# Block 0's second product by seven half products, and a new written order of all work

## The chip, the cores and the metric

The kernel runs on one core of one Trainium2 chip. The metric is the device time of one execution in microseconds; lower is better. The engines are named as in the profile: PE (TensorE matmul; PEld is its weight load), DVE (VectorE), ACT (ScalarE), POOL (GpSimd) and SP (SyncE). Each runs its own instructions in the order in which they are written.

## What is computed

An attention with a window, followed by a two-layer network with a squared ReLU:

```
scores = q @ k.T / sqrt(64) - slope[h] * dist        # 4 batches, 8 heads, 768 positions
keep   = (pos_k < 8) | (0 <= pos_q - pos_k < 96)     # global keys, and a local window
a      = softmax(where(keep, scores, -1e9))
x      = (a @ v), heads side by side                 # 3072 tokens x 512
out    = relu(x @ w_in) ** 2 @ w_out                 # w_in 512 x 2048, w_out 2048 x 512
```

## The kernel before

The 3072 tokens are 24 tiles of 128 (index j), six to a batch. Two tiles make a block (`blk`, 0 to 11). Matmuls run in bf16 and accumulate in eight PSUM banks.

For each tile: loads of q, k and v (q and k of tile 0 come by SP); transposes `tr.n.j` on PE with copies `T.n.j` for tiles 0 to 7, and transposing DMAs for later ones; scores `sc.j` (with a bias matmul `bias.j` for tiles 0 to 2); `exp.j` on ACT; the mask's product `mul.j` on DVE; `pv.j.0` and `pv.j.1`, which multiply by v; `norm.j.0` and `norm.j.1` on DVE, which divide by the row sums; and the transpose of the result, `trx.j` on PE with the copy `xT.j`. `gk`, `gv` and `kl` are small copies of the eight global keys and values.

The first product, x by w_in, has 8 steps of 256 hidden columns. Blocks 0 and 1 do it directly (`s1.blk.s`, L1061; then `relu` and `sq`). For block 0 the steps 0 to 3 are cut by token tile, and steps 0 and 2 also by column half, whose weights are loaded in two pieces, so that `s1.0.0` has four quarters. Blocks 2 to 11 do it by a Strassen-like scheme of seven half products p1 to p7 for each of two groups of steps (`h.blk.g.pN`, L950), with sums of weights `isum` (L888), sums of tokens `xs`, copies `u`, output additions `c` (L995) and squares `q`.

The second product, the squared hidden values by w_out, is direct for block 0 (`s2.0.s.sub`, L1339: 32 matmuls of 512 columns into two banks) and by seven half products for blocks 1 to 11 (`s2.blk.pN.g`, L1212: 8 matmuls of 256 columns for each). The seven-product form needs differences of w_out (`wsum.i.g`, L1132, where g is the half of w_out's steps), sums of the squared hidden values (`sum.blk.i`, L1167), copies of partial results (`part`) and output additions (`o.blk.pN`, L1287). Its banks are two: x takes p1, p6, p7 and p4, and y takes p2, p5 and p3.

Two sets name the blocks that take the seven-product forms:

```
SEVEN = set(range(1, NBLK))      # second product
SEVEN1 = set(range(2, NBLK))     # first product
```

The whole program is laid down in the order of a long string, `ORDER`. Each word is one piece of work; `@A`, `@V` or `@P` picks ACT, DVE or POOL, and `:` gives the PSUM banks. Since every engine works through its own instructions in order, the string sets each engine's queue. On POOL's queue stand the loads (`ld.win.s.c` and `ld.wout.s` for pieces of the weights, `ld.q.j`, `ld.k.j`, `ld.v.j` for tiles 1 to 5, and `load.j` for all three parts of a later tile). SP's queue has the stores and the transposing DMAs.

Of the kernel before, what the change touches and what calls it, by code (L numbers as in the profile page):

```python
# [58 lines left out]
tr.0.1:1 ld.v.0 exp.0.1.0 T.0.1@V sc.1.0 exp.1.0.1 pv.0.0:2 ld.q.2 tr.0.2:3 norm.0.0 ld.k.2 T.0.2@V ld.k.3 exp.1.1.1
pv.0.1:4 tr.1.2:1 bias.2.0:7203 ld.v.1 norm.0.1 exp.1.1.0 ld.q.3 tr.1.3:6 gk.1@A T.1.2@A sc.2.0 exp.1.0.0 T.1.3@V  # L60
ld.k.4 pv.1.0:4 ld.v.2 gk.2@V exp.2.1.0 exp.2.1.1 norm.1.0 trx.0:1 xT.0@A ones.6 pv.1.1:5 tr.0.3:6 T.0.3@V exp.2.0.0
tr.1.4:2 ld.win.6.0 sc.3.0:4361 ld.q.4 norm.1.1 ld.v.3 trx.1:7 gv.1@V exp.2.0.1 exp.3.0.0 pv.2.0:5 exp.3.1.0 exp.3.0.1
T.1.4@V xT.1@V pv.2.1:0 ld.k.5 ld.win.2.0 exp.3.1.1 gk.3@A ld.win.2.1 norm.2.0 s1.0.3:2 mul.3.0 s1.0.6:4 ld.win.4.0
tr.0.4:7 ld.q.5 ld.v.4 norm.2.1 mul.3.1 relu.0.6@A s1.0.3#2 gv.2@P pv.3.0:3 norm.3.0 trx.2:5 T.0.4@A pv.3.1:6
ld.win.1.0 norm.3.1 ld.win.0.1 xT.2@A sc.4.0:1047 exp.4.1.1 exp.4.1.0 tr.1.5:3 T.1.5@A s1.0.2:5 trx.3:6 xT.3@V
ld.win.0.0 ld.win.5.0 s1.0.2#2 s1.0.2#3 s1.0.2#4 relu.0.3@V exp.4.0.1 ld.v.5 gv.3@P exp.4.0.0 gk.4@V sq.0.6@V
relu.0.2@A s1.1.3:7 ld.win.7.0 relu.1.3@A load.6 s1.1.6:0 mul.4.1 tr.0.5:6 mul.4.0 sq.0.3@V s1.1.2:3 T.0.5@A ld.wout.3
pv.4.0:2 ld.wout.1 sq.0.2@V sc.5.0:4157 ld.wout.0 s1.0.4:6 relu.1.2@A exp.5.1.1 s1.0.1:3 sq.1.3@A exp.5.0.0 relu.0.4@V
s1.1.4:7 ld.wout.2 norm.4.0 pv.4.1:4 gv.4@P norm.4.1 sq.0.4@A load.7 exp.5.1.0 sq.1.2@A relu.1.4@A s1.0.0:6 gate.9
ld.wout.4 mul.5.0 s1.0.0#2 sq.1.4@A s1.0.0#3 s1.1.5:2 trx.4:1 exp.5.0.1 relu.1.6@V s1.1.1:4 ld.wout.5 s1.0.1#2  # L70
relu.1.1@A E0.1 mul.5.1 relu.1.5@A pv.5.0:7 s1.1.7:0 s1.1.0:5 sq.1.1@V norm.5.0 ld.wout.6 E0.0 sq.1.5@V tr.1.6:4
sq.1.6@A pv.5.1:2 relu.1.7@A tr.0.6:7 s1.0.0#4 norm.5.1 xT.4@A sq.1.7@A h.2.0.p2:0 ld.wout.7 T.1.6@V h.2.1.p2:1
trx.5:2 xT.5@V relu.1.0@A sq.1.0@A gate.14 h.2.0.p1:5 xs.2.0 s1.0.5:4 sum.1.2 s1.0.7:2 relu.0.1@A xs.2.1 gate.10
sum.1.0 sum.1.1 relu.0.0@A T.0.6@A sc.6.0:36 wsum.0.0 sum.1.3 sq.0.0@A sq.0.1@A s2.0.0.0:7 relu.0.7@A s2.0.1.0 load.9
exp.6.0.0 xs.2.2 s2.0.2.0 exp.6.1.0 s2.0.3.0 s2.0.0.1:2 s2.0.1.1 wsum.2.0 relu.0.5@A sq.0.7@A s2.0.2.1 load.8 mul.6.0
wsum.1.0 s2.0.3.1 tr.0.7:3 tr.1.7:6 gate.15 isum.0.0 h.2.1.p1:4 T.0.7@A s2.0.4.0 isum.0.1 s2.1.p1.0:3 isum.3.1 T.1.7@A
sq.0.5@A pv.6.0:6 isum.1.1 s2.0.4.1 s2.0.5.1 u.2.0.1@A c.2.0.c11 s2.0.5.0 gate.11 u.2.1.1@A h.2.1.p6 q.2.0.c11@A
isum.1.0 T.8 s2.0.6.1 u.2.1.2@A s2.0.6.0 isum.3.0 pv.6.1:0 h.2.0.p6 wsum.2.1 wsum.0.1 s2.1.p1.1 s2.0.7.1 c.2.1.c11
norm.6.0 gate.13 o.0.1@V st.0.1 s2.0.7.0 h.2.1.p7 part.1.p1@A s2.1.p6.0 u.2.0.2@A o.0.0@A u.2.1.3@A h.2.0.p7 h.2.1.p4
T.9 norm.6.1 wsum.3.0 u.2.0.3@A sc.7.0:1762 c.2.1.c21@A wsum.1.1 h.2.1.p5:0 c.2.1.c22 q.2.1.c11@A s2.1.p2.0:4  # L80
exp.7.1.0 exp.7.0.0 isum.2.1 load.10 h.2.0.p4 exp.7.0.1 mul.7.0 exp.7.1.1 s2.1.p2.1 isum.2.0 s2.2.p1.0:7 q.2.1.c21@A
mul.7.1 h.2.0.p5:1 s2.1.p6.1 part.1.p6@A trx.6:6 gate.12 c.2.0.c21@A load.12 pv.7.0:2 xT.6@A c.2.0.c22 q.2.1.c22@A
q.2.0.c22@A s2.2.p1.1 h.2.1.p3 s2.1.p7.0 wsum.3.1 o.1.p2 norm.7.0 h.2.0.p3 pv.7.1:5 s2.1.p7.1 q.2.0.c21@A st.0.0
c.2.1.c12 s2.1.p5.0 s2.1.p5.1 part.1.p7@A q.2.1.c12@A s2.1.p4.0 T.10 s2.1.p4.1 c.2.0.c12 gk.7@V q.2.0.c12@A o.1.p5
o.1.p4@A sc.8.0:6201 st.1.1 part.2.p1@A s2.1.p3.0 norm.7.1 sum.2.0 sum.2.1 s2.1.p3.1 trx.7:5 xT.7@V o.1.p3 h.3.0.p1:3
exp.8.1.0 gk.8@V h.3.1.p1:2 exp.8.0.0 exp.8.1.1 exp.8.0.1 h.3.0.p2:6 xs.3.0 u.3.1.1@A sc.9.0:1540 s2.2.p6.0 mul.8.0
xs.3.1 mul.8.1 u.3.0.1@A h.3.0.p6 exp.9.0.1 exp.9.1.1 gv.7@V h.3.1.p2:4 c.3.0.c11 h.3.1.p6 c.3.1.c11 exp.9.0.0
pv.8.0:0 s2.2.p6.1 pv.8.1:6 load.11 norm.8.0 u.3.1.2@A s2.2.p2.0:1 sum.2.2 gv.8@P q.3.1.c11@A norm.8.1 xT.8 h.3.1.p7
h.3.0.p5:4 u.3.0.2@A h.3.0.p7 s2.2.p2.1 exp.9.1.0 st.1.0 part.2.p6@A xs.3.2 u.3.1.3@A q.3.0.c11@A h.3.1.p5:0 s2.2.p7.0
u.3.0.3@A mul.9.1 mul.9.0 s2.2.p7.1 c.3.1.c22 T.12 c.3.0.c22 pv.9.0:6 h.3.1.p3 o.2.p2 h.3.0.p4 c.3.1.c12 load.15  # L90
norm.9.0 q.3.1.c22@A h.3.0.p3 s2.3.p1.0:5 s2.3.p1.1 c.3.0.c12 q.3.0.c22@A pv.9.1:0 c.3.0.c21@A part.2.p7@A norm.9.1
q.3.1.c12@A h.3.1.p4 q.3.0.c12@A h.4.0.p1:3 c.3.1.c21@A s2.2.p5.0 part.3.p1@A gk.9@V sc.10.0:6402 s2.2.p5.1
q.3.0.c21@A sum.3.0 sum.3.1 s2.2.p4.0 s2.2.p4.1 exp.10.1.0 sum.2.3 exp.10.0.0 exp.10.0.1 h.4.0.p2:4 T.11 u.4.0.1@A
exp.10.1.1 gk.10@V gv.9@A s2.3.p6.0 o.2.p5 mul.10.0 c.4.0.c11 xT.9 h.4.1.p1:6 o.2.p4@A mul.10.1 s2.2.p3.0 s2.2.p3.1
q.3.1.c21@A s2.3.p2.0:0 sum.3.2 u.4.1.1@A pv.10.0:2 pv.10.1:4 s2.3.p6.1 xs.4.0 gate.17 o.2.p3 part.3.p6@A xs.4.1
s2.3.p2.1 norm.10.0 h.4.0.p6 h.4.1.p6 q.4.0.c11@A gv.10@A norm.10.1 u.4.0.2@A load.13 s2.3.p7.0 sc.11.0:7124 u.4.1.2@A
sum.3.3 h.4.0.p7 h.4.1.p7 xs.4.2 exp.11.1.0 o.3.p2 exp.11.0.0 u.4.0.3@V s2.3.p7.1 sc.12.0:17 exp.11.1.1 exp.11.0.1
gate.16 xT.10 h.4.0.p4 c.4.0.c21@A mul.11.0 st.2.0 mul.11.1 h.4.1.p2:4 c.4.1.c11 exp.12.1.0 s2.3.p5.0 pv.11.0:2
pv.11.1:3 s2.3.p5.1 norm.11.0 part.3.p7@A h.4.0.p5:7 q.4.1.c11@A u.4.1.3@A norm.11.1 h.4.1.p5:4 q.4.0.c21@A gate.20
s2.3.p4.0 c.4.0.c22 load.14 s2.3.p4.1 h.4.0.p3 T.13 gate.18 load.16 c.4.1.c22 exp.12.0.0 h.4.1.p4 q.4.1.c22@A h.4.1.p3  # L100
xT.11 s2.4.p2.0:2 h.5.0.p1:3 q.4.0.c22@A o.3.p5 mul.12.0 c.4.0.c12 o.3.p4@A c.4.1.c21@A u.5.0.1@A c.4.1.c12 T.15
s2.3.p3.0 q.4.0.c12@A s2.3.p3.1 q.4.1.c12@V q.4.1.c21@A h.5.0.p2:1 o.3.p3 sc.13.0:5764 st.3.1 st.2.1 h.5.1.p1:0
exp.13.0.0 T.14 s2.4.p2.1 c.5.0.c11 exp.13.1.0 pv.12.1:1 q.5.0.c11@A s2.4.p1.0:5 xs.5.0 sum.4.0 pv.12.0:7 xs.5.1
s2.4.p1.1 mul.13.0 h.5.0.p6 gk.13@V u.5.1.1@A exp.13.0.1 h.5.1.p6 exp.13.1.1 h.5.0.p5:6 sum.4.1 norm.12.0 norm.12.1
h.5.1.p2:4 xs.5.2 mul.13.1 c.5.1.c11 h.5.1.p5:7 u.5.1.2@A sum.4.2 gate.19 part.4.p1@A h.5.1.p7 u.5.0.2@A h.5.0.p7
o.4.p2 u.5.0.3@A c.5.0.c22 pv.13.0:1 u.5.1.3@A norm.13.0 s2.4.p6.0 s2.4.p6.1 xT.12 st.3.0 q.5.1.c11@A T.16 part.4.p6@A
h.5.0.p4 pv.13.1:4 s2.4.p5.0 sum.4.3 c.5.0.c21@A h.5.0.p3 h.5.1.p4 q.5.0.c22@A s2.4.p7.0 norm.13.1 s2.4.p7.1 s2.4.p5.1
c.5.0.c12 q.5.0.c21@A kl.15@V part.4.p7@A c.5.1.c22 q.5.0.c12@A sc.14.0:1346 o.4.p5 s2.4.p4.0 xT.13 exp.14.0.1 kl.14@V
h.5.1.p3 gv.13@P q.5.1.c22@V c.5.1.c12 c.5.1.c21@A s2.4.p4.1 load.17 h.6.0.p1:4 s2.4.p3.0 s2.4.p3.1 exp.14.1.1
exp.14.1.0 exp.14.0.0 sc.15.0:0673 mul.14.1 mul.14.0 xs.6.0 o.4.p4@A xs.6.1 h.6.0.p2:1 o.4.p3 q.5.1.c12@A s2.5.p1.0:5  # L110
u.6.0.1@A c.6.0.c11 exp.15.0.0 exp.15.1.0 exp.15.1.1 sum.5.0 s2.5.p1.1 h.6.0.p6 u.6.0.2@A exp.15.0.1 sum.5.1 load.18
h.6.0.p5:2 part.5.p1@A pv.14.0:0 norm.14.0 pv.14.1:6 h.6.1.p1:1 u.6.1.1@A h.6.0.p7 gv.14@P st.4.0 s2.5.p6.0 u.6.0.3@A
# [1319 lines left out]
```

## Time and profile before

| What | Value |
|---|---|
| Median of 3 runs | 199.83 us (199.76 to 200.56) |
| Span of the profiled execution, first to last instruction | 197.6 us |
| What lies between that span and the median | 2.2 us |
| PE, DVE, ACT, POOL busy | 97%, 88%, 82%, 41% |
| Granted clock of PE | 1.00 |
| DMA moved | 26.91 MB, mean 136 GB/s |

The profiled execution has no time of its own beside its span; its span is set against the median. Busy shares are means over the whole span; the stages differ, and the rows by stage say which engine is full where. The landing of a load is its issue on POOL's queue plus the time that the view of transfers gives.

### The profile page before, as it was taken

The page shows a single profiled execution, that of the slowest core. Times are in us where ns is not written, and L with a number is a line of the kernel's source. Part 1 is how long each engine was busy: PE and PEld are TensorE (multiplying, and loading weights), DVE is VectorE, ACT ScalarE, POOL GpSimd, SP SyncE. Part 2 cuts the span into 40 slices and gives each one's busy share as a digit, 9 for nine tenths or more (in the row PEclk, how much of TensorE's full clock was granted, in tenths as well). Part 3 has the DMA queues.
Part 4 walks back from the last instruction along what each step waited for, and adds up shares of the span by engine and source line. Part 5 has one row for each costly group of instructions (what it writes and reads, how often), then busy time and mean ns, then how long its engine had stood idle before and what let it go on. Part 6 is the DMA issues. An engine that isn't in the chain of part 4 may idle for free.

```text
span 197.6 us, 6777 instructions
## 1 busy us (share of the span) xinstructions
PE 191.9 (97%) x2776; PEld 169.6 (86%) x2776; DVE 173.2 (88%) x423; ACT 163.0 (82%) x335; POOL 80.4 (41%) x101
## 2 busy tenths in 40 slices
...
GB/s 127 153 158 171 181 181 185 182 202 159 139 209 191 75 200 88 145 174 210 151 129 203 114 124 194 160 121 92 136 81 116 154 55 56 27 30 163 0 106 106
DMA packets 111857, 26.91 MB, mean 136 GB/s; under 512 B 103379, under 2 KB 109011, under 8 KB 111827
## 3 DMA queue, kind: packets, MB, share of 16 engines
...
## 4 chain that ended last, share of the span: by engine, by line
PE 95%; DVE 2%; issue 1%; ACT 0%; DVEq 0%
PE bank L1212 35%; PE bank L950 32%; PE bank L1061 7%; PE bank L599 6%; PE bank L748 5%; PE bank L1339 4%; PE bank L372 2%; PE bank L506 2%; PE bank L532 1%; DVE qkT L433 1%; PE bank L816 1%; PE bank L579 0%; ACT qkT L429 0%; DVE o L1287 0%; DVE v L433 0%
## 5 line engine op out<-in xcount | busy, mean ns | idle before, releaser
L1015 ACT ACTIVATE hs<-hr 128x512 bf16<-128x512 f32 x72 | 44.8, 641 | 5.1 <-DVE hr L995 4.7
L665 ACT ACTIVATE esc<-bank 128x512 bf16<-128x512 f32 x78 | 42.9, 614 | 1.3 <-PE bank L599 1.0
L1212 PE MATMUL bank<-wsum,hsum 128*128 128x256 bf16 x264 | 36.2, 273 | 0.0
L1212 PEld LDWEIGHTS <-hsum 128*128 128x128 bf16 x360 | 32.1, 98 | 4.1 <-issue 0.5
L995 DVE CUSTOM_DVE_ANT_0 hr<-bank,early 128x512 f32<-128x512 f32 x45 | 30.4, 685 | 2.5 <-PE bank L950 1.5
L950 PEld LDWEIGHTS <-win 128*128 128x128 bf16 x480 | 29.7, 98 | 1.0
L950 PEld LDWEIGHTS <-qk_first 128*128 128x128 bf16 x480 | 29.7, 98 | 1.0
L429 ACT COPY early<-bank 128x512 f32<-128x512 f32 x42 | 24.5, 591 | 3.6 <-PE bank L950 3.3
L690 DVE TENSOR_TENSOR at<-esc,E 128x1024 bf16<-128x1024 bf16 x39 | 26.7, 696 | 0.1
L1212 PEld LDWEIGHTS <-hs 128*128 128x128 bf16 x264 | 24.0, 98 | 2.6
L310 POOL DMA_DIRECT2D qk<-in_q_dram x18 | 16.0, 890 | 21.9 <-DMA qkT<-qk 20.6
L1212 PE MATMUL bank<-wout,hs 128*128 128x256 bf16 x176 | 24.9, 273 | 0.0
L310 POOL DMA_DIRECT2D v<-in_v_dram x18 | 16.0, 888 | 18.3 <-DVE v L480 14.9
L950 PE MATMUL bank<-xT,win 128*128 128x128 bf16 x320 | 23.4, 219 | 0.0
L431 POOL COPY v<-v 8x520 bf16<-8x520 bf16 x8 | 5.7, 718 | 43.3 <-PE bank L748 43.3
L950 PE MATMUL bank<-xs,qk_first 128*128 128x128 bf16 x320 | 22.8, 219 | 0.0
L779 DVE TENSOR_TENSOR x<-bank,rs 128x256 bf16<-128x256 f32 x48 | 20.4, 425 | 1.7
L865 ACT ACTIVATE hr<-bank 128x512 f32<-128x512 f32 x33 | 19.4, 598 | 1.3 <-PE bank L950 0.4
L748 PE MATMUL bank<-v,at 128*128 128x65 bf16 x352 | 17.8, 193 | 0.0
L1287 DVE TENSOR_TENSOR o<-bank,part 128x256 f32<-128x256 f32 (+2 forms) x34 | 13.8, 410 | 3.3 <-PE bank L1212 3.2
L429 ACT COPY part<-bank 128x256 f32<-128x256 f32 x29 | 10.9, 375 | 7.1 <-PE bank L1212 6.9
L310 POOL DMA_DIRECT2D qk<-in_k_dram x18 | 16.1, 897 | 0.9 <-DMA win<-in_moe_w_in_dram 0.5
...
## 6 DMA issues: line engine op xcount, KB each, us to landing
out_dram<-o SPq DMA_DIRECT2D x22, 256.0 KB, 2.5
v<-in_v_dram POOLq DMA_DIRECT2D x24, 128.0 KB, 5.6
qk<-in_q_dram POOLq DMA_DIRECT2D x18, 128.0 KB, 5.0
qk<-in_k_dram POOLq DMA_DIRECT2D x18, 128.0 KB, 5.8
wout<-in_moe_w_out_dram POOLq DMA_DIRECT2D x8, 256.0 KB, 8.5
win<-in_moe_w_in_dram POOLq DMA_DIRECT2D x6, 256.0 KB, 6.9
qk_first<-in_k_dram POOLq DMA_DIRECT2D x5, 128.0 KB, 5.6
qk_first<-in_q_dram POOLq DMA_DIRECT2D x5, 128.0 KB, 5.7
```

The source lines that it names most:

```text
L310: nc.gpsimd.dma_start(out=dst, in_=src)
L429: nc.scalar.copy(dst, src)
L665: nc.scalar.activation(out=tiles[tag, j, g][:, odd], in_=tiles.pop(("sc", j, odd, g)).rearrange("p a c -> p (a c)"), func=Act.Exp, scale=s ...
L690: nc.vector.tensor_mul(at, tiles.pop(("esc", j, g)), bias)
L748: nc.tensor.matmul(out=po[:, hi, :], lhsT=tiles["at", j, g][:, odd, at * P : (at + 1) * P], rhs=v_sb[kj][:, h, :], start=(i == 0), stop=(i ...
L779: nc.vector.tensor_tensor(out=x[:, 4 * hf : 4 * hf + 4, :], in0=po[:, :, :D], in1=rs.to_broadcast([P, 4, D]), op=Alu.mult,)
L865: nc.scalar.activation(dst, src, Act.Relu)
L950: nc.tensor.matmul(out=tiles["h", blk, g, bank][:, n], lhsT=left_[:, s, k], rhs=right_[:, k], start=opens and n == 0 and k == 0, stop=k == ...
L995: nc.vector._custom_dve(TENSOR_ADD_SAT, out=hr, in0=src, in1=tiles.pop(("u", blk, g, i)), s0=float("inf"), s1=0.0,)
L1015: nc.scalar.activation(hs, hr, Act.Square)
L1061: nc.tensor.matmul(out=hT[:, c, cols], lhsT=w_in_sb[s][:, kt, c * P : (c + 1) * P], rhs=tiles["xT", blk][:, kt, cols], start=(kt == 0), st ...
L1212: nc.tensor.matmul(out=tiles["acc", blk, bank][:, cols], lhsT=left_[:, s], rhs=right_[:, cols], start=first and s == 0, stop=s == NSTEP - ...
```

## The change

The second product of block 0 joins the seven-product form, and the string `ORDER` is replaced as a whole. Nothing else differs. The new file is one line shorter, so all its line numbers after the string are lower by one.

```diff
 ORDER = """
-tr.0.0:0 warm:7 tr.1.0:1 T.1.0@V bias.0.0:23 T.0.0@A sc.0.0 ld.win.3.0 exp.0.0.0 ld.k.1 tr.1.1:4 bias.1.0:5670 T.1.1@V ld.q.1
+ld.q.1 ld.q.2 ld.q.3 ld.win.4.0 ld.v.1 ld.k.1 ld.v.0 ld.q.4 ld.win.2.0 ld.k.2 tr.0.1:5 tr.0.0:4 warm:6 tr.1.1:2 T.1.1@V
...
-    SEVEN = set(range(1, NBLK))
+    SEVEN = set(range(0, NBLK))
```

Block 0's second product so goes from 32 matmuls of 512 columns to 56 of 256, and gains four `sum`, three `part`, three output additions and one output copy in place of two output copies of 512 columns. Of all `part` copies 11 instead of 4 are on DVE. All three early copies `gv` that POOL had among the loads (tiles 2, 3 and 4) go to DVE.

On POOL, the loads of the opening. Before, from the first load of v that follows q of tile 5 (v_75 is v of tile 4, v_76 of tile 5, v_77 and v_78 of tiles 6 and 7; L431 is a copy `gv`):

```order
L307 DMA v_75<-in_v_dram 128x8x64
L431 COPY v_73<-v_71 8x8x65
L307 DMA win<-in_moe_w_in_dram 128x4x256
L307 DMA win<-in_moe_w_in_dram 128x4x128 x2
L307 DMA win<-in_moe_w_in_dram 128x4x256
L307 DMA v_76<-in_v_dram 128x8x64
L431 COPY v_74<-v_71 8x8x65
L307 DMA win<-in_moe_w_in_dram 128x4x256
L310 DMA v_77<-in_v_dram 128x8x64
```

After, from v of tile 4 on; ahead of it stand all three loads of tile 7 and of tile 6:

```order
L306 DMA v_75<-in_v_dram 128x8x64
L306 DMA wout<-in_moe_w_out_dram 128x2x512 x3
L306 DMA win<-in_moe_w_in_dram 128x4x256 x2
L306 DMA v_76<-in_v_dram 128x8x64
L306 DMA wout<-in_moe_w_out_dram 128x2x512
L306 DMA win<-in_moe_w_in_dram 128x4x256
L306 DMA wout<-in_moe_w_out_dram 128x2x512
L306 DMA win<-in_moe_w_in_dram 128x4x128 x2
L306 DMA wout<-in_moe_w_out_dram 128x2x512 x3
```

The last of w_in (two half pieces, step 0) moved from ahead of tiles 6 and 7 to behind them and behind five pieces of w_out; those two were loads 22 and 23 of the queue, with step 7 as the last of w_in at load 26, and are loads 36 and 37 now. The last of w_out is load 40 in both.

On DVE, the place where the differences of w_out are made for its upper half. Before (L1132 `wsum`, L995 `c`, L778 and L779 `norm`, L433 the output copy of block 0):

```order
L888 TENSOR_TENSOR qk_first<-qk_first,win 128x1024
L888 TENSOR_TENSOR plain<-win 128x1024
L1132 TENSOR_TENSOR wsum_97<-wout 128x1024
L1132 TENSOR_TENSOR wsum_95<-wout 128x1024
L995 ISA hr<-bank_108,early 128x512
L778 RECIPROCAL rs<-bank_113 128x4
L779 TENSOR_TENSOR x<-bank_113,rs 128x256
L480 MEMSET v_74 128x1
L433 COPY o<-bank_109 128x512
```

After (L1131 `wsum`, L1166 `sum` of block 0, L1286 the output addition of p2 of block 0, L887 `isum`):

```order
L1131 TENSOR_TENSOR wsum_95<-wout 128x1024
L1131 TENSOR_TENSOR wsum_96<-wout,wsum_95 128x1024
L1131 TENSOR_TENSOR wsum_97<-wout 128x1024
L1166 TENSOR_TENSOR hsum<-hs 128x1024
L1166 TENSOR_TENSOR hsum<-hsum,hs 128x1024
L1131 TENSOR_TENSOR wsum_98<-wout,wsum_96 128x1024
L1286 TENSOR_TENSOR o<-bank_108,part 128x256
L1166 TENSOR_TENSOR hsum<-hs 128x1024
L887 TENSOR_TENSOR qk_first<-qk_first,win 128x1024
```

The sums of block 0 now stand directly behind three `wsum` of the upper half of w_out. On PE the seven products of block 0 follow directly on the first pieces of block 2: `h.2.0.p2 trx.5 h.2.0.p1 s2.0.p1.0 s2.0.p1.1 s2.0.p2.0 s2.0.p2.1 sc.6.0 s2.0.p6.0`, behind `s1.0.0` (four quarters), `pv.5.1`, `s1.1.0` and `s1.1.7`.

More of the change, by code (lines that the diff above doesn't have):

```diff
@@ L57 @@
 ORDER = """
-tr.0.0:0 warm:7 tr.1.0:1 T.1.0@V bias.0.0:23 T.0.0@A sc.0.0 ld.win.3.0 exp.0.0.0 ld.k.1 tr.1.1:4 bias.1.0:5670 T.1.1@V ld.q.1
[L59 to L112, printed above, removed]
@@ new lines @@
+ld.v.3 ld.q.5 ld.k.3 ld.v.2 E0.0 E0.1 T.0.2@V tr.0.3:5 tr.1.2:4 pv.1.0:3 sc.0.0 T.1.2@V norm.1.0 exp.0.1.0 gk.1@A
+exp.0.0.0 ld.k.4 ld.k.5 ld.win.3.0 ld.win.6.0 ld.win.2.1 pv.1.1:6 bias.2.0:3204 gv.1@A T.0.3@A pv.0.0:1 sc.2.0 pv.0.1:7
+norm.1.1 ones.6 norm.0.0 norm.0.1 tr.1.3:6 T.1.3@V exp.2.1.1 trx.1:4 trx.0:7 exp.2.1.0 gk.2@A exp.2.0.0 sc.3.0:2516
+xT.0@V xT.1@V pv.2.0:7 exp.2.0.1 exp.3.0.0 exp.3.1.0 s1.0.3:3 pv.2.1:4 norm.2.0 norm.2.1 gv.2@V mul.3.0 load.7 load.6
+ld.v.4 tr.0.4:2 s1.0.6:0 s1.0.3#2 exp.3.1.1 exp.3.0.1 T.0.4@A trx.2:4 pv.3.0:2 xT.2@A relu.0.3@A relu.0.6@A tr.1.4:6
```

144 lines of the change are left out of this document (96 added, 48 removed).

## The prediction, made before the changed kernel was run

> **What bounds the kernel now.** First the busy shares on the page, then busy time by stage, then the chain of waits.
>
> ```profile
> span 197.6 us, 6777 instructions
> PE 191.9 (97%) x2776; PEld 169.6 (86%) x2776; DVE 173.2 (88%) x423; ACT 163.0 (82%) x335; POOL 80.4 (41%) x101
> 18.00:40.00 22.00, 22.00 (x323) 19.59 (x320) 19.04 (x48) 20.61 (x41) 18.39 (x25) 1.00 1.80 182
> 40.00:60.00 20.00, 20.00 (x244) 15.62 (x243) 19.65 (x45) 16.33 (x34) 10.10 (x13) 1.00 1.64 177
> 60.00:188.00 128.00, 128.00 (x1979) 118.29 (x1978) 119.90 (x276) 111.77 (x231) 34.74 (x41) 1.00 1.09 122
> PE 95%; DVE 2%; issue 1%; ACT 0%; DVEq 0%
> ```
>
> In a stage's row stand its ends and length, then busy time of PE, PEld, DVE, ACT and POOL, granted clock, DMA share, GB/s. From 18 us on PE is never idle and 95% of the chain is PE. So the time is the opening, plus the matmuls, plus a short end: a wait put into PE's queue after 18 us is not won back. Two more things: DVE is nearly as full between 40 and 60 us (19.65 of 20), and the loads run at 177 to 182 GB/s through the first 60 us.
>
> **PE's own work.** The direct second product of block 0 is 32 matmuls of 512 columns; a seven-product form is 7 times 8 matmuls of 256 columns.
>
> ```profile
> 34.62 0.24 PE bank L748 x8
> 34.86 0.22 PE bank L506 x4
> 35.08 0.22 PE bank L1061 x4
> 35.31 0.89 PE bank L950 x16
> 36.20 0.26 PE bank L816 x4
> 36.46 0.45 PE bank L950 x8
> 36.91 1.75 PE bank L1061 x16
> 38.66 0.33 PE bank L599 x8
> 38.99 3.56 PE bank L1339 x16
> 42.55 0.45 PE bank L506 x8
> 50.69 0.55 PE bank L599 x16
> 52.68 0.87 PE bank L1212 x8
> ```
>
> These are pieces of the chain: start, length, what (L1061 and L950 first products, L1339 and L1212 second products, L748 pv, L506 and L816 transposes, L599 scores). L1339: two times 3.56 = 7.1 us go. L1212: seven times 0.87 = 6.1 us come. PE saves 1.0 us, all of it on the path, if the new work finds its operands ready.
>
> **Where the last of w_in stands in POOL's queue.** Counting the loads on POOL's queue, before has the last piece of w_in as load 26 and the last of w_out as load 40. After has win.0.0 and win.0.1 as loads 36 and 37, behind tiles 6 and 7, v of tile 5 and five pieces of w_out; the last of w_out is again load 40. The first 37 loads are the same set by kind in both (22 of q, k or v, ten pieces of w_in, five of w_out), so I take the landing of load number n from before.
>
> ```profile
> 1.34 0.89 POOL L307 DMA_DIRECT2D win<-in_moe_w_in_dram  x1 [0.17 <-issue]
> 2.22 0.90 POOL L307 DMA_DIRECT2D qk_first<-in_k_dram  x1
> 3.10 0.90 POOL L307 DMA_DIRECT2D qk_first<-in_q_dram  x1
> 18.33 0.62 POOL L431 COPY v<-v 8x520 bf16<-8x520 bf16 x1
> 18.89 2.98 POOL L307 DMA_DIRECT2D win<-in_moe_w_in_dram  x4
> 23.27 0.76 POOL L307 DMA_DIRECT2D win<-in_moe_w_in_dram  x1
> 26.30 0.88 POOL L310 DMA_DIRECT2D qk<-in_k_dram  x1 [0.52 <-DMA win<-in_moe_w_in_dram]
> 34.29 1.49 POOL L307 DMA_DIRECT2D wout<-in_moe_w_out_dram  x2
> 37.61 0.71 POOL L307 DMA_DIRECT2D wout<-in_moe_w_out_dram  x1 [0.58 <-DMA wout<-in_moe_w_out_dram]
> win<-in_moe_w_in_dram POOLq DMA_DIRECT2D x1, 256.0 KB, 5.7
> win<-in_moe_w_in_dram POOLq DMA_DIRECT2D x1, 256.0 KB, 7.7
> wout<-in_moe_w_out_dram POOLq DMA_DIRECT2D x1, 256.0 KB, 8.2
> wout<-in_moe_w_out_dram POOLq DMA_DIRECT2D x1, 256.0 KB, 8.7
> ```
>
> The last four are the view of transfers narrowed to one issue each; the last figure is us from issue to landing, for loads 1, 26, 37 and 40. So load 26 lands at 23.27 + 7.7 = 31.0, load 37 at 34.29 + 8.2 = 42.5, load 40 at 37.61 + 8.7 = 46.3. The delay grew from 5.7 to 8.7, and POOL itself stands still for earlier transfers (0.52, 0.58): the transfers, not the issue, set this pace.
>
> What stands behind it on PE: after's s1.0.0 needs load 36 for its first quarter and load 37 for its second, and its remaining three quarters (0.22 each), pv.5.1 (0.24), s1.1.0 and s1.1.7 (1.75 together) come next in PE's order: all of the first product of blocks 0 and 1 is done at 42.5 + 0.66 + 0.24 + 1.75 = 45.15. Before reaches the end of that work at 36.91 + 1.75 = 38.66, with 0.89 + 0.45 of block 2 (L950) and 0.26 of trx.5 (L816) done as well and the transposes of tile 7 (L506, 0.45) still to do; for the same work that is 38.66 - 1.60 + 0.45 = 37.51. PE is 7.64 us late, and nothing later has idle time to take it up.
>
> The opening is late too, but hidden: after's s1.0.3 needs win.3, now load 17, where before began L1061 at 18.29.
>
> ```profile
> 14.23 2.38 POOL L307 DMA_DIRECT2D win<-in_moe_w_in_dram  x3
> win<-in_moe_w_in_dram POOLq DMA_DIRECT2D x2, 128.0 KB, 6.0
> 18.29 1.32 PE bank L1061 x16
> ```
>
> Loads 16 and 17 go out at 14.23 and some 0.75 later, 6.0 to landing, so win.3 is there at 21.0: 2.7 us late with 0.46 less attention work done. That lies ahead of the wait for load 37; its cover is that wait, and if the cover is gone it costs 3.2.
>
> Three copies of v (0.62 each) leave POOL's queue. If POOL set the pace, load 37 would land 1.9 sooner; if the transfers do, 0. I take 0.5, nearer to the transfers' end because of the waits on them.
>
> **The sums of block 0 on DVE.** Four sums, three output adds and some copies come to DVE. In DVE's order wsum.0.1, wsum.1.1, wsum.2.1 (which need all of w_out, load 40), sum.0.0 and sum.0.1 follow one another, and s2.0.p6 on PE needs sum.0.1.
>
> ```profile
> 46.36 0.68 DVE L888 TENSOR_TENSOR plain<-win 128x1024 bf16<-128x1024 bf16 x1
> 46.96 1.28 DVE L1132 TENSOR_TENSOR wsum<-wout 128x1024 bf16<-128x1024 bf16 x2
> 48.17 0.68 DVE L995 CUSTOM_DVE_ANT_0 hr<-bank,early 128x512 f32<-128x512 f32 x1
> 56.16 0.42 DVE L1287 TENSOR_TENSOR o<-bank,part 128x256 f32<-128x256 f32 x1
> 56.49 0.17 DVE L778 RECIPROCAL rs<-bank 128x4 f32<-128x4 f32 x1
> ```
>
> Big DVE operations start 0.605 apart (46.36, 46.96, 48.17 with two between) and take 0.68; an output add costs 0.33 of the queue. From load 40 at 46.3: sum.0.1 starts 4 x 0.605 later and ends at 49.4. PE after 45.15 has two pieces of h.2.0 and trx.5 (1.15), s2.0.p1 and p2 (0.87 each) and sc.6 (0.33): it stands at p6 at 48.4 and waits 1.0. Going on in the same way (p5 waits for the output add of p2, which reads its bank: 0.1; pv.6.1 for mul.6.0, nine DVE operations after sum.0.1: 0.35; trx.7 for norm.7.1, 21.7 us of DVE's queue behind load 40: 0.4) PE loses 1.9 in all. Bounds: 0, if PE is so late that DVE is ahead, and 3.7, which is 1.9 plus the same again, since each of these waits rests on a queue of ten to forty operations.
>
> After 60 us DVE was idle for 128 - 119.90 = 8.1 us; the copies of part and v that move to it there are about 2.5 us (eleven part copies instead of four, at 0.33 of the queue each, as for an output add). I cost them at nothing under that idle time; without the cover they cost up to 2.5. The end of the program changes by one output add that no longer stands between two pieces of p3, 0.2 at most; left out.
>
> Sum: 7.64 late loads, less 0.5 for POOL's copies, less 1.0 of PE work, plus 1.9 waits on DVE = +8.0. Against the span of 197.6 that gives 205.6; the runs shown have a median of 199.83, 2.2 above that span for what lies outside it, so 207.8.
>
> **Rivals.**
> (1) The loads come sooner by the full 1.9 and DVE's waits are swallowed by PE's lateness: 7.64 - 1.9 - 1.0 + 0.5 (a rest of DVE's waits) = +5.2, 205.0. For it: POOL's three copies stood among the loads; against it: POOL's waits on transfers.
> (2) DVE stays behind: the 2.5 us of moved copies are not covered, because PE has no slack after 60 us and each late operand shows: +10.5, 210.3. For it: DVE at 19.65 of 20 up to 60 us. Against: 8.1 us idle later.
> (3) Only the opening counts: the w_in loads land in time and 3.2 - 1.0 = +2.2 remains, 202.0. Against: load 37 would have to land about 5 us sooner.
> (4) Not slower: no load holds PE up, 1.0 us of matmuls is saved, 198.8. Without waits POOL could issue load 37 near 31 (0.88 for each of 22 loads, 0.74 for each piece of w_in, 0.71 for each of w_out, after 1.34). PE has 16.1 us of work between its first L1061 and s1.0.0 (13 steps of the first product at 0.87, two sc at 0.55, ten groups of transposes at 0.22, six pv at 0.24), so from 18.3 it arrives at 34.4. This decides if load 37 lands within 3.4 us of its issue. The first load, with an empty queue, took 5.7, and the later ones shown took longer.
> The Trainium skill, page "DMA: Bandwidth & Descriptors", section "Anatomy of one DMA — SWDGE (gpsimd) path", gives a load from GpSimd as about 2.0 us plus its bytes over 436 GB/s. By that rule, as an estimate, a 256 KB load would take 2.6 us and rival (4) would hold. The trace disagrees, with 5.7 to 8.7 for loads in a queue.
>
> **Chances.** Forecast as summed (206 to 209.5): 0.55. Rival (1) 0.20, rival (2) 0.15, rival (3) 0.06, rival (4) 0.04. The likeliest gives 207.8; the range 204.0 to 211.0 takes in (1) and (2) and the bounds of 0 and 3.7 for DVE's waits, and leaves out (3), (4) and the far tail of (2), under 0.2. A measurement of this kernel tells about 0.5%, 1.0 us, from no change. Rival (4) sits just at that line and is split: faster 0.02, same 0.02; everything else is slower, 0.96.
>
> **What would show it.** Right: the last first-product matmul of blocks 0 and 1 ends near 45 instead of 38.7; PE has idle time between 20 and 45 us, ended by DMA of win; wsum and the block 0 sums on DVE run from about 46; from 70 us on the rows of PE look as before, some 8 us later. Wrong: w_in's last piece lands before 38 us, or PE is busy throughout 30 to 45 us. The forecast fails low if loads 26 to 40 land faster than in before, and high if DVE, not PE, releases most of what ends late after 70 us.

## The result, and the profile after

| | before | after |
|---|---|---|
| Median | 199.95 us (199.76 to 200.56, 4 runs) | 210.68 us (209.95 to 210.81, 4 runs) |
| Span of the profiled execution | 197.6 us | 208.2 us |
| Ratio after to before | | 1.053, 95% interval 1.049 to 1.057 |

The change makes the kernel 10.7 us slower. The forecast was 207.8 with a range of 204.0 to 211.0: right in sign and inside the range, 2.9 us too low. The profiled execution of after has the shortest span of the four (208.2 to 209.0 us). An execution more than 1.5% above the fastest of its kernel is left out of the times given here (e4, e7 and e9 to e12 have such). First the head of the page of after: span, busy shares, the granted clock in 40 slices, and the shares of the chain of waits.

```profile
span 208.2 us, 6824 instructions
PE 193.6 (93%) x2800; PEld 172.2 (83%) x2800; DVE 176.0 (85%) x430; ACT 164.6 (79%) x341; POOL 78.1 (38%) x97
PEclk9969999999999999999999999999999999999999
PE 63%; POOL 13%; DMA 11%; DVE 9%; issue 2%; DVEq 0%; POOLq 0%
```

PE's share of the chain fell from 95% to 63%. POOL with its loads, and DMA, now hold 24% of it. Busy time by stage says when (ends and length, then busy time of PE, PEld, DVE, ACT, POOL, the granted clock, the DMA share, GB/s):

```profile
30.00:45.00 15.00, 12.22 (x163) 10.47 (x164) 10.61 (x26) 11.56 (x23) 10.38 (x13) 1.00 1.46 195
45.00:60.00 15.00, 13.44 (x183) 11.90 (x182) 13.46 (x32) 11.11 (x24) 1.90 (x3) 1.00 0.90 70
60.00:72.00 12.00, 12.00 (x177) 10.73 (x175) 11.86 (x28) 10.71 (x23) 5.98 (x7) 1.00 1.85 171
72.00:198.00 126.00, 125.28 (x1924) 115.65 (x1923) 117.86 (x272) 108.76 (x225) 31.79 (x37) 1.00 0.97 119
```

Before, PE was full from 18 us on. After, it stands idle for 2.8 us between 30 and 45 and for 1.6 between 45 and 60, and is nearly full again from 60. The four longest groups of PE's waits by what they waited for (total, times, longest), and rows of PE's timeline:

```profile
PE bank L505 <- DMA qk_first<-in_k_dram: 2.6, 1, 2.6
PE bank L1060 <- DMA win<-in_moe_w_in_dram: 2.1, 2, 1.8
PE bank L505 <- DMA qk_first<-in_q_dram: 1.4, 1, 1.4
PE bank L1211 <- DVE hsum L1166: 1.3, 1, 1.3
```

```profile
34.87 1.05 PE L1060 MATMUL bank<-xT,win 128*128 128x256 bf16 x8 [1.82 <-DMA win<-in_moe_w_in_dram]
40.40 1.03 PE L1060 MATMUL bank<-xT,win 128*128 128x256 bf16 x8 [0.48 <-DVE x L778]
41.74 0.40 PE L1060 MATMUL bank<-xT,win 128*128 128x128 bf16 x4 [0.31 <-DMA win<-in_moe_w_in_dram]
42.48 0.84 PE L1060 MATMUL bank<-xT,win 128*128 128x128 bf16 x12
45.15 0.61 PE L949 MATMUL bank<-xT,win 128*128 128x128 bf16 x8
46.27 1.91 PE L1211 MATMUL bank<-wout,hs 128*128 128x256 bf16 x16
49.81 1.97 PE L1211 MATMUL bank<-wsum,hsum 128*128 128x256 bf16 x16 [1.30 <-DVE hsum L1166]
```

PE waits for pieces of w_in at 34.87 and 41.74, takes up the second quarter of `s1.0.0` at 42.48, and begins block 2 (L949) at 45.15, so the first products of blocks 0 and 1 are done there. The row at 49.81 is the other predicted wait: p6 of block 0 for `sum.0.1` on DVE. Loads 37 and 40 on POOL, the view of transfers narrowed to load 37 (8.7 us from issue to landing), and on DVE the first `wsum` of the upper half of w_out, which waits for load 40, and `sum.0.1`:

```profile
33.76 0.74 POOL L306 DMA_DIRECT2D win<-in_moe_w_in_dram  x1 [0.52 <-DMA wout<-in_moe_w_out_dram]
37.29 0.70 POOL L306 DMA_DIRECT2D wout<-in_moe_w_out_dram  x1
win<-in_moe_w_in_dram POOLq DMA_DIRECT2D x1, 128.0 KB, 8.7
46.41 0.69 DVE L1131 TENSOR_TENSOR wsum<-wout 128x1024 bf16<-128x1024 bf16 x1 [1.37 <-DMA wout<-in_moe_w_out_dram]
49.06 0.69 DVE L1166 TENSOR_TENSOR hsum<-hsum,hs 128x1024 bf16<-128x1024 bf16 x1
```

**Where the 10.6 us of span went.** One point compares like with like: the first product of block 3 that follows `trx.7` and `s2.1.p3`. Up to there PE has done the same steps in both kernels, but for the two forms of block 0. The first row is of before, the second of after.

```profile
60.69 1.50 PE L950 MATMUL bank<-xT,win 128*128 128x128 bf16 x24
69.51 1.50 PE L949 MATMUL bank<-xT,win 128*128 128x128 bf16 x24
```

After is 8.8 us late here. The other 1.8 come behind it: from this point to the end of the span before takes 197.6 - 60.69 = 136.9 us, after 208.2 - 69.51 = 138.7. The rows of the stretch from here to the end of PE's last matmul, before and after (columns as above):

```profile
60.69:194.85 134.16, 133.71 (x2035) 123.30 (x2032) 123.54 (x286) 113.95 (x236) 34.05 (x40) 1.00 1.04 121
69.51:204.57 135.06, 134.34 (x2034) 123.67 (x2031) 123.62 (x286) 112.99 (x235) 32.21 (x38) 1.00 0.93 118
```

So the 1.8 has two halves: 0.9 up to the last matmul, and another 0.9 behind it, where the last additions and stores run (197.6 - 194.85 = 2.75 us before, 208.2 - 204.57 = 3.6 after). Two questions were left for the chip: what makes the 8.8, and what the 1.8.

### The profile page after: what moved, and what is told of

Its sections match the earlier page's. It is cut to its first block, busy times and chain, and to the rows that moved or that the text cites. A ratio compares the mean times of both kernels' runs of the same rounds, so it can differ in the third digit from the quotient of the medians.

```text
span 208.2 us, 6824 instructions
## 1 busy us (share of the span) xinstructions
PE 193.6 (93%) x2800; PEld 172.2 (83%) x2800; DVE 176.0 (85%) x430; ACT 164.6 (79%) x341; POOL 78.1 (38%) x97
## 4 chain that ended last, share of the span: by engine, by line
PE 63%; POOL 13%; DMA 11%; DVE 9%; issue 2%; DVEq 0%; POOLq 0%
PE bank L1211 31%; PE bank L949 25%; DMA wout<-in_moe_w_out_dram 4%; DMA win<-in_moe_w_in_dram 4%; POOL qk_first L306 4%; PE bank L598 4%; PE bank L747 4%; DMA xT<-x 3%; POOL win L306 2%; POOL v L306 2%; DVE at L689 2%; POOL qk L309 2%; DVE hr L994 2%; POOL wout L306 1%; DVE wsum L1131 1%
## 5 line engine op out<-in xcount | busy, mean ns | idle before, releaser
L1211 PE MATMUL bank<-wsum,hsum 128*128 128x256 bf16 x288 | 39.1, 273 | 1.4 <-DVE hsum L1166 1.3
L1211 PEld LDWEIGHTS <-hsum 128*128 128x128 bf16 x392 | 35.2, 98 | 5.8 <-DVE hsum L1166 1.8
L949 PEld LDWEIGHTS <-qk_first 128*128 128x128 bf16 x480 | 29.7, 98 | 1.0 <-DVE xs L921 0.2
L949 PEld LDWEIGHTS <-win 128*128 128x128 bf16 x480 | 29.7, 98 | 0.9
L1211 PEld LDWEIGHTS <-hs 128*128 128x128 bf16 x288 | 26.3, 98 | 2.7
L1211 PE MATMUL bank<-wout,hs 128*128 128x256 bf16 x192 | 26.8, 273 | 0.0
L689 DVE TENSOR_TENSOR at<-esc,E 128x1024 bf16<-128x1024 bf16 x39 | 25.9, 683 | 0.7 <-ACT esc L664 0.7
L309 POOL DMA_DIRECT2D v<-in_v_dram x18 | 16.6, 921 | 20.0 <-DVE rs L777 13.2
L949 PE MATMUL bank<-xT,win 128*128 128x128 bf16 x320 | 23.4, 219 | 0.0
L949 PE MATMUL bank<-xs,qk_first 128*128 128x128 bf16 x320 | 23.3, 219 | 0.0
L430 POOL COPY v<-v 8x520 bf16<-8x520 bf16 x4 | 3.0, 745 | 51.9 <-PE bank L747 51.9
L778 DVE TENSOR_TENSOR x<-bank,rs 128x256 bf16<-128x256 f32 x48 | 20.4, 424 | 1.7
L1060 PE MATMUL bank<-xT,win 128*128 128x256 bf16 (+1 forms) x160 | 16.3, 252 | 2.9 <-DMA win<-in_moe_w_in_dram 2.1
L1286 DVE TENSOR_TENSOR o<-bank,part 128x256 f32<-128x256 f32 (+2 forms) x37 | 15.1, 410 | 4.2 <-PE bank L1211 4.2
L747 PEld LDWEIGHTS <-at 128*128 128x128 bf16 x352 | 15.6, 98 | 2.7 <-DVE at L689 1.2
```

The source lines that it names most:

```text
L309: nc.gpsimd.dma_start(out=dst, in_=src)
L689: nc.vector.tensor_mul(at, tiles.pop(("esc", j, g)), bias)
L747: nc.tensor.matmul(out=po[:, hi, :], lhsT=tiles["at", j, g][:, odd, at * P : (at + 1) * P], rhs=v_sb[kj][:, h, :], start=(i == 0), stop=(i ...
L778: nc.vector.tensor_tensor(out=x[:, 4 * hf : 4 * hf + 4, :], in0=po[:, :, :D], in1=rs.to_broadcast([P, 4, D]), op=Alu.mult,)
L949: nc.tensor.matmul(out=tiles["h", blk, g, bank][:, n], lhsT=left_[:, s, k], rhs=right_[:, k], start=opens and n == 0 and k == 0, stop=k == ...
L1211: nc.tensor.matmul(out=tiles["acc", blk, bank][:, cols], lhsT=left_[:, s], rhs=right_[:, cols], start=first and s == 0, stop=s == NSTEP - ...
```

## The experiments

e1 to e4 asked whether the place of the loads, the form of block 0 or the copies on DVE make the loss; e5 and e7 to e12 take the early causes away one after the other; e6 sizes one term in the kernel before. All edits are given in words of the string `ORDER`. Letters name theories, which the expectations explain. Line numbers differ by one or two between the kernels. A kernel's mark is the start of the product of block 3 at which before and after were just compared.

**e1_win_early: w_in back to the front of POOL's queue.** After, with POOL's queue alone changed.

```diff
-ld.q.1 ld.q.2 ld.q.3 ld.win.4.0 ... load.7 load.6 ld.v.4 ld.wout.1 ... ld.win.0.0 ld.win.0.1 ld.wout.6 ld.wout.4 ld.wout.7
+ld.win.3.0 ld.k.1 ld.q.1 ld.v.0 ... ld.win.0.1 ld.win.0.0 ld.win.5.0 ld.v.5 ld.win.7.0 ... load.7 load.6 ld.wout.1 ... ld.wout.7
```

> The changed kernel, with only POOL's queue of loads altered: all of w_in and tiles 1 to 5 in the order of before (last of w_in is load 26 again), then tiles 7 and 6, then all of w_out, whose last piece stays load 40. Theory A (two gates one behind the other: w_in's last piece at 42.5, and w_out's last piece, which s2.0.p1.1 and wsum.0.1 need at 46.3): the first product of blocks 0 and 1 is done near 38 us, but PE then stands at s2.0.p1.1 until 46.3; time 209 to 211, no real gain. Rival B (the place of w_in's loads is what costs, as the prediction put it): PE runs on from 38 us, time 203 to 205.

Measured: 212.84 us (211.80 to 213.58), ratio 1.064 (1.058 to 1.070), two us slower than after and above what either theory said. PE's largest wait, its row, and the two stretches that follow:

```profile
PE bank L1061 <- DVE x L779: 4.7, 1, 4.7
42.82 2.29 PE L1061 MATMUL bank<-xT,win 128*128 128x256 bf16 x12 [4.73 <-DVE x L779]
40.00:45.00 5.00, 2.18 (x13) 1.68 (x13) 4.04 (x10) 0.99 (x2) 3.48 (x4) 0.58 1.31 201
45.00:50.00 5.00, 5.00 (x58) 4.67 (x56) 3.84 (x9) 4.18 (x9) 0.00 (x0) 0.73 2.28 150
```

PE now has w_in, and waits for `norm.5.0` (L779) on DVE, which frees its bank. In DVE's order `norm.5.0` stands behind `wsum.2.0` and `wsum.0.0`, which need pieces of w_out, and those are the last loads now. So w_in's place alone is not the cause: in after's order of work w_out gates PE too, as theory A said, but at `norm.5.0` through DVE and not at `s2.0.p1.1`. Behind the wait the granted clock falls (0.58 and 0.73 on the mean of these stretches), which adds to the price.

**e2_before_late_loads: after's load order in the kernel before** (and its three copies `gv` on DVE).

```diff
-ld.win.3.0 ld.k.1 ld.q.1 ...
+ld.q.1 ld.q.2 ld.q.3 ld.win.4.0 ... load.7 load.6 ld.v.4 ld.wout.1 ... ld.wout.7
-gv.2@P gv.3@P gv.4@P
+gv.2@V gv.3@V gv.4@V
```

> The kernel before, with only the changed kernel's order of loads on POOL's queue (and the three early copies gv of tiles 2 to 4 on DVE instead of POOL, so that they don't stand among the loads). Theory A (late loads cost what PE's order leaves uncovered): s1.0.0 stands until load 37 lands at 42.5 instead of starting near 31, so +10 to +12: 210 to 212. Rival C (the new order and the seven products, not the loads, make the time): within 2 us of before, 200 to 202.

Measured: 214.71 us (214.27 to 215.45), ratio 1.076 (1.070 to 1.081).

```profile
PE bank L1059 <- DMA win<-in_moe_w_in_dram: 7.3, 3, 4.2
35.00:40.00 5.00, 3.18 (x24) 2.49 (x24) 0.87 (x5) 1.20 (x3) 1.97 (x3) 0.50 1.48 197
40.00:45.00 5.00, 3.48 (x27) 2.79 (x28) 2.35 (x5) 0.52 (x2) 0.91 (x1) 0.56 1.40 194
```

The load order alone, in the kernel that has block 0 direct and its work in the old order, costs 15 us, where A said 10 to 12: PE waits 7.3 for w_in, and the matmuls behind that run at about half clock (0.50 and 0.56). The late loads are enough to make a loss of the size seen. After, with the same first 40 loads, takes 4.0 us less, so the rest of the change hides part of their lateness.

**e3_parts_on_act: the eleven `part` copies of blocks 1 to 10 that after has on DVE go to ACT.**

```diff
-part.1.p7@V part.3.p7@V part.4.p7@V part.5.p1@V ... part.10.p7@V
+part.1.p7@A part.3.p7@A part.4.p7@A part.5.p1@A ... part.10.p7@A
```

> The changed kernel with all eleven part copies that stand on DVE put on ACT. Theory D (the 1.8 us that PE loses between 72 and 135 us is DVE's queue, lengthened by these copies): 1 to 2 us less, 208.7 to 209.7. Rival E (those losses come from where the words stand, or ACT becomes late in turn): 210.2 or more.

Measured: 213.09 us (212.78 to 214.51), ratio 1.068 (1.063 to 1.074), 2.4 us more than after. Two waits are new:

```profile
PE bank L949 <- ACT hr L864: 0.8, 1, 0.8
PE bank L1211 <- ACT part L428: 0.4, 1, 0.4
```

ACT is the late one instead, as E said. So the copies on DVE are not a loss that can be had back by moving them, with the rest of this order as it is.

**e4_direct_block0: block 0 direct again, everything else as in after.** The 32 matmuls stand at the places of the seven products.

```diff
-    SEVEN = set(range(0, NBLK))
+    SEVEN = set(range(1, NBLK))
-s2.0.p1.0:4 s2.0.p1.1 s2.0.p2.0:1 s2.0.p2.1 ... sum.0.0 ... part.0.p1 ... o.0.p2
+s2.0.0.0:4 s2.0.1.0 s2.0.0.1:1 s2.0.1.1 ...
```

> The changed kernel with the second product of block 0 direct again, its 32 matmuls put at the places of the seven products; loads and all else as in the changed kernel. Theory A (loads first, then the sums of block 0 on DVE): 1.0 us more matmuls, less the 2.0 us that PE waits for DVE between 45 and 60 us, less up to 1 us later: 208.5 to 210. Rival F (the seven products of block 0 themselves cause the loss): 203 or less.

Measured: 211.29 us (210.29 to 211.64), ratio 1.057 (1.051 to 1.063). This cannot be told from after; it lies 1.3 above A's upper end, and far from F's 203. The form named in the change is not what costs; the order is.

**e5_both_early: w_in early as in e1, then all of w_out, then tiles 6 and 7**, whose transposes move behind `s2.0.p2` and `s2.0.p5` (the copy `T.0.6` also goes from DVE to ACT).

```diff
-... load.7 load.6 ld.v.4 ld.wout.1 ... ld.win.0.0 ld.win.0.1 ... ld.wout.7
+... ld.win.0.1 ld.win.0.0 ld.win.5.0 ld.v.5 ld.win.7.0 ... ld.wout.1 ... ld.wout.7 load.6 load.7
```

> The changed kernel with both weights early: POOL's queue has w_in and tiles 1 to 5 in the order of before (last of w_in is load 26), then all of w_out (loads 27 to 34, landing by about 40), then tiles 6 and 7 (loads 35 to 40); the four transposes of tiles 6 and 7 move behind s2.0.p2 and s2.0.p5 on PE, so that they don't stand and wait ahead of the first product. Theory A2 (w_in and w_out both gate PE, the latter also through DVE's queue, where wsum.2.0 stands ahead of norm.5.0): with both gone the products of block 0 start near 40 instead of 46.3, time 204 to 206.5. Rival G (the loss is in the new order of words on PE and DVE, whatever the loads): 208 or more.

Measured: 207.98 us (207.49 to 208.76), ratio 1.043 (1.040 to 1.046): 2.7 us gained on after, where A2 said 4 to 7. G's limit was 208, so the time does not refute it.

```profile
43.61 1.91 PE L1211 MATMUL bank<-wout,hs 128*128 128x256 bf16 x16
PE bank L505 <- DMA qk_first<-in_q_dram: 4.0, 1, 4.0
PE bank L598 <- ACT qkT L428: 0.9, 1, 0.9
```

The first of the seven products starts at 43.61 instead of 46.27, 2.7 us sooner; the transposes of tiles 6 and 7 (two times 0.45) have moved behind it, and at the mark (67.53) 2.0 are left. So both weights together gate less than A2 said. The opening is one reason: PE waits 4.0 us there, as in after (1.4 for q and 2.6 for k), and no late piece of w_in stands behind to cover it. A new wait for ACT comes later.

**e6_before_parts: the kernel before with after's eleven `part` copies on DVE.**

```diff
-part.1.p7@A part.3.p7@A ... part.5.p7@V ... part.7.p1@V ...
+part.1.p7@V part.3.p7@V ... part.5.p7@A ... part.7.p1@A ...
```

> The kernel before, with the same eleven part copies on DVE as in the changed kernel (four in before). This measures by itself the term that the prediction costed at nothing. If DVE's idle time covers them: 199.3 to 200.4. If not (rival 2 of the prediction): 201 to 202.5.

Measured: 201.11 us (199.65 to 201.55, 7 runs) against 199.53 for before: ratio 1.008 (1.005 to 1.010), 1.5 us. The profiled execution, the fastest of the seven, has its mark row here:

```profile
59.78 1.50 PE L949 MATMUL bank<-xT,win 128*128 128x128 bf16 x24
```

From there to the end of its span are 197.7 - 59.78 = 137.9 us, 1.0 more than in before. Its mark comes 0.9 sooner than that of before, although the order is the same up to there: the eight warm-up matmuls of the opening took 1.89 us in this execution and 2.62 in that of before. A mark can thus shift by 0.9 from one execution to the next. Moving the copies costs 1.0 to 1.5 us with nothing else changed.

**e7_both_early_opening: e5 with before's written order up to the first `s1.0.3`.**

```diff
-(the opening of after, up to s1.0.3)
+(the opening of before, up to s1.0.3)
```

> The kernel e5 (both weights early), with the opening, all words up to the first piece of s1.0.3, in the order of before. Theory A2: the opening's lateness of 2.7 to 3.2 us, which the late loads hid, shows once they are early, so this gains 2 to 3 us on the kernel with both weights early: 201.5 to 204. Rival H (the opening is covered by another wait, such as tile 6's landing): less than 1 us gained.

Measured: 209.21 us (207.92 to 210.13), ratio 1.048 (1.043 to 1.053), no gain on e5. That is H's time, but not for the cause that H named:

```profile
37.92 2.27 PE L1060 MATMUL bank<-xT,win 128*128 128x256 bf16 x12 [3.47 <-DVE x L778]
36.03 1.29 DVE L1131 TENSOR_TENSOR wsum<-wout 128x1024 bf16<-128x1024 bf16 x2 [3.63 <-DMA wout<-in_moe_w_out_dram]
```

PE comes sooner and stands at e1's place: DVE waits 3.63 us for w_out with `norm.5.0` behind it, and PE waits 3.47 for that.

**e8_e7_direct_block0: e7 with block 0 direct, as in e4.** The edit is that of e4.

> The kernel e7 with block 0's second product direct again at the same places. This prices the seven products where no load of weights holds them up: 1.0 us more matmuls, four sums and three adds less on DVE. If the saving of matmuls arrives, this is 0.5 to 1.0 us slower than e7; if DVE is the bound there, it is equal or up to 2 us faster.

Measured: 208.07 us in one execution and 211.89 to 213.05 in three, too far apart for a verdict; e11 asks the question again.

**e9_no_wsum_gate: e7 with three `wsum` moved on DVE, behind the work that PE waits for.**

```diff
-pv.5.0:2 wsum.2.0 wsum.0.0 s1.0.1#2 norm.5.0 s1.0.5:6 s1.0.7:2 wsum.1.0 isum.0.0 isum.0.1 isum.1.1 ... norm.5.1
+pv.5.0:2 s1.0.1#2 norm.5.0 s1.0.5:6 s1.0.7:2 isum.0.0 isum.0.1 isum.1.1 ... wsum.2.0 wsum.0.0 wsum.1.0 norm.5.1
```

> Kernel e7 with three differences of w_out (wsum.2.0, wsum.0.0, wsum.1.0) moved on DVE from ahead of norm.5.0 to ahead of norm.5.1, so that neither norm.5.0 nor the sums of w_in stand behind a load of w_out. Nothing else differs. Theory A3 (in e7 DVE waited 3.63 us for w_out with norm.5.0 behind it, and PE so waited 3.47 us for a bank and then ran at a lower clock): that wait of PE goes, the loads then gate only the seven products of block 0 from about 43 us, of which some 1 to 2 us of waiting stays; 205 to 207 us. Rival J (the wait only moves: PE comes 3.5 us earlier to the products that need w_out, and stands there instead): 208 to 210, with PE's longest wait between 18 and 50 us at the second product (L1211) or at the sums of w_in (L949), over 2 us.

Measured: 205.65 and 206.58 us, against 198.97 for before; two times are too few for an interval, and e12 repeats this run. The profiled execution took 206.58, with a span of 204.7:

```profile
39.22 0.61 PE L949 MATMUL bank<-xT,win 128*128 128x128 bf16 x8
40.49 1.94 PE L1211 MATMUL bank<-wout,hs 128*128 128x256 bf16 x16
43.81 0.62 PE L505 MATMUL bank<-ident,qk 128*128 128x128 bf16 x8 [1.37 <-DMA qk<-in_k_dram]
45.37 0.40 PE L598 MATMUL bank<-qkT 64*128 64x128 bf16 x8 [0.94 <-ACT qkT L428]
66.00 1.50 PE L949 MATMUL bank<-xT,win 128*128 128x128 bf16 x24
```

The wait of 3.47 is gone. The first products of blocks 0 and 1 end at 39.2 instead of 45.15; 0.9 of that are the transposes moved behind them, so 5.0 of the 7.64 us are back. At the mark 69.51 - 66.00 = 3.5 are left of it. New waits take the rest: k of tile 6, now at the end of the same queue, is missed at 43.81, and its copy on ACT at 45.37. A3's mechanism held, and both times lie in its range of 205 to 207. J's wait of over 2 us is not there, but smaller ones are, for other data.

**e10_before_part_engines: e9 with the `part` copies of blocks 1 to 11 on before's engines.** The edit is the reverse of that of e6.

> Kernel e9 with the part copies of blocks 1 to 11 on the engines that before gave them (four on DVE, the rest on ACT); those of block 0 stay where after has them. Against e9. Theory K (the seven copies more on DVE cost about 1.5 us, as they did in before): 1 to 2 us less than e9. Rival L (the rest of the order was laid out around them; with the copies on ACT, ACT's queue is late instead, as when all eleven went there): no gain or up to 2.5 us more, with new waits of PE for ACT (hr, part).

Measured: 209.76 and 212.55 us, ratio 1.059 (1.049 to 1.070), slower than e9. PE waits for `relu` (0.7 us) and `part` (0.4) on ACT, as in e3. Its mark:

```profile
65.54 1.58 PE L949 MATMUL bank<-xT,win 128*128 128x128 bf16 x24
```

From the mark to the end it takes 208.0 - 65.54 = 142.5 us, e9 204.7 - 66.00 = 138.7. Theory K is refuted: in before's order the copies are better on ACT, in after's on DVE.

**e11_e9_direct_block0: e9 with block 0 direct**, and **e12_e9_once_more: e9 unchanged**, on one chip. The edit of e11 is that of e4.

> Kernel e9 with block 0's second product direct, its 32 matmuls of 512 columns at the places of the seven products, without the sums and part copies of block 0. Compared with e9 on the same chip. Theory M (once the loads come early the form itself costs nothing but PE's own work): about 1.0 us more than e9, since the direct form is 7.1 us of PE instead of 6.1. Rival N (the seven products wait for sums, part copies and banks, and load DVE where it is full): 0.5 to 2 us less than e9.

> The text of e9 unchanged, on the same chip as its direct variant, for the comparison of the two; e9's executions lay between 205.65 and 209.71. If its usual time is 205.5 to 206.7, the gain over the changed kernel is 4 to 5 us; if 207.5 to 209.7, it is 1 to 3.

Measured: e11 208.25 us (207.88 to 210.53), ratio 1.048 (1.043 to 1.053); e12 207.68 (206.70 to 208.89), ratio 1.044 (1.040 to 1.047). The direct form takes 0.6 us more by the medians. That has the sign of theory M (about 1.0), but the two intervals overlap; N's gain is not there. e12 falls into its upper band, a gain of 3.0 us on after; single executions of e9's text reach 205.65, and the section on the hardware shows one cause of such differences.

## Why the prediction was right in sign and 2.9 us low

The 2.9 are 2.6 of span (10.6 measured, 8.0 forecast) and 0.3 between span and median. The 2.6 are 0.5 for POOL's copies, 0.3 ahead of the mark and 1.8 behind it.

**PE's own work, -1.0: held as far as the runs tell.** The direct form takes 0.6 us more in e11 than in e12, and 0.6 more in e4 than in after. Both lie inside the spread of the runs, and both hold the waits that each form brings along.

**Load 37, +7.64 us for the first products: held.** The prediction took the landing by the number of the load: 42.5. PE takes up that quarter at 42.48, and block 2 begins at 45.15, as summed. e2 shows that the load order alone makes such a loss (more of it, 15 us; before's PE comes to it sooner and loses its clock). As a price the 7.64 hold for after's path alone: with this wait and the other early ones gone, in e9, only 3.5 of the 8.8 at the mark come back, because new waits take their place.

**The late opening, hidden: held.** `s1.0.3` could not begin before win.3, forecast for 21.0, and begins at 21.41. The page's PEclk row dips to 6 in the third slice, behind a wait of 2.6 us for k, and nothing of that shows at 45.15. e5 shows the reverse: with the wait for load 37 gone, the opening's 4.0 us of waiting are no longer covered.

**POOL's copies, -0.5: wrong, it was 0.** Load 37 was issued at 33.76, half a microsecond sooner than the 34.29 that the prediction had from before, and took 8.7 us where load 37 of before took 8.2, so it landed at 42.5 all the same. The transfers set the landing, as the waits on POOL had said; the prediction read that and still took half a microsecond. (Its 177 to 182 GB/s hold for 18 to 60 us, the stages that it shows, and not for the first 60 us; no term hangs on that.)

**DVE behind load 40, +1.9 in all: held in sum.** Load 40 landed by 46.41 (forecast 46.3), `sum.0.1` ended at 49.75 (49.4), p6 waited 1.3 (1.0), and `pv.6.1` 0.3 for `mul.6.0` (0.35). The waits put down for p5 and `trx.7`, 0.5 together, do not show in the trace, so that the sum is this close is partly luck. At the mark the kernel is 8.8 us late; 7.64 - 1.0 + 1.9 = 8.5. The 0.3 left over is not assigned; it is less than the 0.9 by which a mark can shift (e6).

**What lies behind the mark, put at nothing: the step that failed.** After loses 1.8 us there. The prediction had two terms for this stretch, and both were off.

The first is the copies moved to DVE: 2.5 us of them, at nothing under 8.1 us of DVE's idle time. It counted what comes to DVE and not what leaves. The new order also takes copies such as `gk.9`, `gk.10`, `kl.14` and `xT.7` and some squares off DVE, and from the mark to the last matmul DVE runs 286 instructions in both kernels, 123.54 us before and 123.62 after. So DVE got no more to do, and the cover was not called on. Whether it would have held is another question, and e6 answers it: there the copies do come on top (124.96 us of DVE in the same stretch), and they cost 1.0 to 1.5 us although DVE is idle for 10.6 of the 134.16 us. An average of idle time is no cover.

After's PE still loses 0.9 us up to the last matmul. Of that, 0.3 is waiting that shows: 0.72 against 0.45 before (which is one wait at its end, see below). The largest wait is 0.59, at 86.92, where the chain of waits leads back over DVE to a transposing DMA that was issued behind a norm on DVE. The other is 0.14, behind a `part` copy:

```profile
79.30 5.52 DMA xT<-x
85.58 1.30 DVE at L689 x2
86.92 0.42 PE bank L747 x8
118.37 0.42 DVE part L432
```

The remaining 0.6 is spread over the matmuls in steps too short to show as waits, and its cause stays open: e3 and e10 took the copies away and met ACT, so no run shows after without them and without a new wait.

The second term is the end, 0.2 at most and left out. Behind the last matmul after takes 0.9 us more. Its order puts the last output additions (`o.11.p3`, two pieces) behind all of p3 and the last three stores behind both; before has one addition and one of these stores ahead of the last piece of p3. PE there waits 0.45 for the addition, which after saves, so the new end costs some 0.4 net. e6, which has before's end, loses nothing behind its last matmul.

Rival (2) has 210.3, the nearest number to the result, but by luck: it charges 2.5 for copies that do not add to DVE's work. DVE does not release most of what ends late, as the prediction asked of this failure, but its share of the chain is 9% instead of 2%.

**The rivals.** (1) needed load 37 some 1.9 sooner, (3) 5 sooner and (4) 8; it came when the forecast said. Load 37, of 128 KB, took 8.7 us from issue to landing. The Trainium skill, page "DMA: Bandwidth & Descriptors", section "Anatomy of one DMA — SWDGE (gpsimd) path", would give 2.3 as an estimate, and the trace disagrees for a load in a queue.

**What the prediction did not see.** It treated w_in as the only gate of the first products. e1 and e7 show a second one at the same place: `norm.5.0` on DVE stands behind two `wsum`, so loads of w_out hold PE up even when w_in is there. In after it shows for 0.48 us only, at 40.40. And e9 has a third: with both gone, the loads put last in the queue, those of tile 6, come at 43.8, and PE is there before them. The table gives each kernel's mark and its remainder:

| kernel | mark | span | mark to end |
|---|---|---|---|
| before | 60.69 | 197.6 | 136.9 |
| after | 69.51 | 208.2 | 138.7 |
| e5, both weights early | 67.53 | 206.6 | 139.1 |
| e9, and DVE's gate gone | 66.00 | 204.7 | 138.7 |
| e10, e9 with before's copies | 65.54 | 208.0 | 142.5 |
| e6, before with after's copies | 59.78 | 197.7 | 137.9 |

What helps ahead of the mark leaves the loss behind it as it was, 1.8 to 2.2. No version tried comes near before, with block 0 in either form. e9's mark is still 5.3 us behind before's. Its trace has 4.9 us of waits in six places between 18 and 50 us, where PE in before has none: 1.8 for a norm on DVE at 20.73, 2.6 for k of tile 6 and for copies of transposes on ACT from 43 us on, and 0.5 for relus. No run took these away.
